# Writing each engine's order of work out as a list, in place of priorities that a small scheduler weighs

## The chip, the cores and the metric

One Trainium2 chip, one core. The metric is the device time of one execution in microseconds (us), smaller is better. In the profile PE is the engine of the matmuls, PEld its weight loads, DVE, ACT and POOL are the vector, scalar and GpSimd engines, and SP issues transfers; SPq is SP's transfer queue. The span of a trace runs from its first to its last instruction; in the kernels timed here the measured time is 1.8 to 2.1 us more than the span (median of each kernel's executions).

## The reference, cut to what matters

```python
# attention part: 4 batches, 8 heads, 768 steps, 48 wide
f = 1 / (1 + exp(-f_logit))
for t in range(S):
    state = f[t] * state + outer(k[t], v[t])
    y[t]  = q[t] @ state
# MLP part: x = y as 3072 tokens of 384
h   = x @ w_in                       # 384 -> 2048
g   = 0.5 * (h + sqrt(h*h + 4))
out = g @ w_out                      # 2048 -> 384
```

All inputs and the output are float32; the kernel multiplies in float16.

## The kernel before

It cuts the 3072 steps into 24 blocks of 128 steps, two blocks to a pair, 12 pairs. For each pair it loads f, q, k and v (eight loads of 192 KB), takes logs of the decays, sums them with matmuls, takes exponentials, multiplies q and k by them, transposes, and makes scores, states and y. Then y is transposed and goes through the two layers of the MLP: "first-layer" groups (M1: 6 matmuls, then a square and, for two groups together, one root on ACT, then the gate on DVE) and "second-layer" quarters (M2). The weights come in eight pieces each of w_in and w_out, issued by POOL between its own products and casts.

ACT needs another table of functions for exponentials than for roots (the trace has twelve table loads of 1.28 us; around the one at 57.68 us a root ends at 57.66 and the exponential starts at 58.97), so it works in stretches of one kind.

Every piece of work is an `Op` with an engine, its needs and the code that emits it. A small model of the chip runs in the builder and decides in what order each engine's instructions are written down. In the kernel before, it chooses among what is ready by a due time, made of one number per pair and part and one per kind:

```python
BASE = {
    "A": [108.49, 34.87, 152.35, -8.64, ...],        # logs, decays, q*e, k*e, casts
    "B": [-110.5, 81.39, 112.94, 46.29, ...],        # attention
    ...
    "L": [-402.69, -47.56, -326.02, -208.05, ...],   # loads
}
SHIFT = {"ldf": -73.74, "ldq": 12.88, ..., "pin": -578.98, "pout": -533.94, ...}
NEAR = {'PE': 0.02, 'ACT': 0.05, 'DVE': 0.2, 'POOL': 0.3, 'SP': 0.1}
# [...]
    def run(self):
        # [...] cands: the first op of every queue of the engine, with the time it could start
                t0 = min(c[0] for c in cands)
                near = [c for c in cands if c[0] <= t0 + NEAR.get(eng, 0.05)]
                c = min(near, key=lambda c: c[1].due)
```

Transposes are done by PE for the early pairs and by a transfer that transposes for the later ones, both of q and k (`qkT`) and of y (`xT`, the input of the first layer).

```python
                def yx():
                    xn()
                    nc.sync.dma_start_transpose(out=xo(), in_=T["y16", r].rearrange("p a b -> p (a b)"))
                op = P.add("xy", "SP", 1.2, yx, deps=[yc_op], p=p, due=due + 6.0, ...)
```

These transposes stand in the same queue of SP as the loads.

## Time and profile before

| | before |
|---|---|
| time, median of 3 executions | 207.05 us (206.78 to 207.27) |
| span of the profiled execution | 205.7 us (that execution took 207.66 us) |
| busy: PE, ACT, DVE, POOL | 180.6, 168.9, 144.0, 90.7 us |
| mean transfer rate over the span | 156 GB/s |

The lines that carry the argument are shown in the prediction: the busy table and slices, unbroken runs of matmuls, and the chain of waits from 15 to 45 us.

### The profile page before, as it was taken

What the parts mean: (1) busy time and instruction counts of PE and PEld (TensorE: products, weight loads), DVE (VectorE), ACT (ScalarE), POOL (GpSimd) and SP (SyncE); (2) the same over time, 40 slices, a digit from 0 to 9 for tenths busy, and PEclk for the clock granted to TensorE, in tenths of its full rate; (3) what the DMA queues carried; (4) which work ended last, traced back from release to release, by engine and by line L of the source; (5) the groups of instructions that cost most, each with busy time, mean ns of one, the idle gap of its engine ahead of it and who ended that gap; (6) DMA issues with size and microseconds to landing.
All of it is one profiled execution on the core that took longest, in us unless ns stands there. A gap on an engine that the chain in (4) does not pass through costs nothing.

```text
span 205.7 us, 4831 instructions
## 1 busy us (share of the span) xinstructions
PE 180.6 (88%) x1870; PEld 131.7 (64%) x1870; DVE 144.0 (70%) x286; ACT 168.9 (82%) x271; POOL 90.7 (44%) x103
## 2 busy tenths in 40 slices
PE   0666588769898998999999999999989999999993
PEld 0343365557676576777777777677757777767751
DVE  5856276778765768998598984989718988943720
ACT  5457217979999999999999999999879899967930
POOL 7171699990049396309960059900079100010010
PEclk9999996999999999999999999999999999999999
DMA  7999999999799999999999897998967712031112
GB/s 129 189 186 184 183 189 183 201 201 191 134 208 212 188 214 188 197 178 223 207 163 217 139 206 147 202 184 170 195 138 153 132 36 62 21 96 41 38 38 76
DMA packets 128102, 32.09 MB, mean 156 GB/s; under 512 B 121088, under 2 KB 127360, under 8 KB 128080
## 3 DMA queue, kind: packets, MB, share of 16 engines
q1 hardware_dynamic: 121744, 25.70, 74.4%
q0 software_dynamic: 6336, 6.10, 15.2%
q8 instruction: 14, 0.23, 0.5%
q14 instruction: 8, 0.07, 0.1%
HBM read 25.17 MB, written 4.72 MB: 145 GB/s over the span
## 4 chain that ended last, share of the span: by engine, by line
PE 60%; ACT 11%; DMA 9%; SPq 7%; POOL 5%; issue 3%; DVE 3%; DVEq 0%; ACTq 0%; POOLq 0%
PE o L777 26%; PE hps L734 23%; SPq L376 7%; ACT r L749 4%; DMA w_in<-in_moe_w_in_dram 4%; ACT hsq L740 3%; DMA ld_q<-in_q_dram 3%; PE sc L612 3%; DMA xT<-y 2%; POOL w_in L400 2%; PE y L635 1%; PE u L700 1%; PE y L633 1%; ACT ld_f L422 1%; PE u L697 1%
## 5 line engine op out<-in xcount | busy, mean ns | idle before, releaser
L734 PE MATMUL hps<-xT,w_in 128*128 128x256 f16 x576 | 72.3, 276 | 2.6 <-DMA w_in<-in_moe_w_in_dram 2.0
L757 DVE SCALAR_TENSOR_TENSOR g<-hps,r 128x512 f16<-128x512 f32 x96 | 62.1, 685 | 17.4 <-ACT r L749 16.6
L777 PE MATMUL o<-w_out,g 128*128 128x384 f16 x384 | 72.3, 326 | 0.9 <-DVE o_sb L788 0.8
L734 PEld LDWEIGHTS <-w_in 128*128 128x128 f16 x576 | 55.1, 99 | 14.0 <-DMA w_in<-in_moe_w_in_dram 3.0
L740 ACT ACTIVATE hsq<-hps 128x512 f16<-128x512 f32 x96 | 54.0, 591 | 6.8 <-PE hps L734 5.5
L749 ACT ACTIVATE r<-hsq 128x1024 f16<-128x1024 f16 x48 | 50.8, 1057 | 1.4
L777 PEld LDWEIGHTS <-g 128*128 128x128 f16 x384 | 35.3, 97 | 20.2 <-issue 1.3
L619 DVE TENSOR_TENSOR pm<-sc,mask 128x512 f16<-128x512 f32 x48 | 31.3, 683 | 8.8 <-PE sc L612 8.6
L792 POOL DMA_DIRECT2D out_dram<-o_sb x15 | 8.6, 571 | 59.1 <-DVE o_sb L788 43.4
L484 POOL TENSOR_TENSOR qk<-ld_q,ea 128x768 f16<-128x768 f32 (+1 forms) x10 | 15.7, 1571 | 27.1 <-PE hps L471 14.2
L484 POOL TENSOR_TENSOR qk<-ld_k,eap 128x768 f16<-128x768 f32 (+1 forms) x12 | 18.6, 1546 | 0.7 <-ACT eap L478 0.6
L433 POOL TENSOR_TENSOR llo<-ls,lhi 128x768 f16<-128x768 f32 (+1 forms) x12 | 16.8, 1399 | 2.0 <-PE hps L734 1.5
L491 POOL CAST v<-ld_v 128x768 f16<-128x768 f32 (+1 forms) x13 | 8.8, 682 | 18.5 <-DMA ld_v<-in_v_dram 17.6
L704 DVE TENSOR_TENSOR sn<-u,gam 128x384 f16<-128x384 f32 x20 | 11.0, 551 | 7.3 <-PE u L700 6.7
L422 ACT ACTIVATE ld_f<-ld_f 128x768 f32<-128x768 f32 (+1 forms) x15 | 10.8, 723 | 4.6 <-DMA ld_f<-in_f_logit_dram 4.5
L478 ACT ACTIVATE ea<-hps 128x384 f32<-128x384 f32 x24 | 10.9, 500 | 4.1 <-PE hps L471 4.0
L464 PE MATMUL hps<-lhi,wcent 128*128 128x384 f16 x24 | 8.7, 361 | 6.1 <-POOL lhi L430 5.4
L635 PE MATMUL y<-v,pm 128*128 128x48 f16 x192 | 12.0, 189 | 1.0 <-DVE pm L619 1.0
L635 PEld LDWEIGHTS <-pm 128*128 128x128 f16 x192 | 10.4, 100 | 2.9 <-DVE pm L619 1.1
L612 PE MATMUL sc<-qkT 48*128 48x128 f16 x192 | 10.6, 233 | 1.8 <-DVE qkT L591 0.8
L587 PE MATMUL tr<-ident,qk 128*128 128x128 f16 x80 | 7.8, 256 | 4.7 <-POOL qk L484 4.3
L427 ACT ACTIVATE ls<-ld_f 128x768 f32<-128x768 f32 (+1 forms) x15 | 10.7, 715 | 1.0
(55 smaller groups left out, 209.0 us busy)
## 6 DMA issues: line engine op xcount, KB each, us to landing
ld_f<-in_f_logit_dram SPq DMA_DIRECT2D x24, 192.0 KB, 4.6
ld_k<-in_k_dram SPq DMA_DIRECT2D x24, 192.0 KB, 4.6
ld_q<-in_q_dram SPq DMA_DIRECT2D x24, 192.0 KB, 4.4
ld_v<-in_v_dram SPq DMA_DIRECT2D x24, 192.0 KB, 4.3
out_dram<-o_sb POOLq DMA_DIRECT2D x15, 192.0 KB, 3.6
out_dram<-o_sb SPq DMA_DIRECT2D x9, 192.0 KB, 2.0
w_in<-in_moe_w_in_dram POOLq DMA_DIRECT2D x8, 192.0 KB, 7.1
w_out<-in_moe_w_out_dram POOLq DMA_DIRECT2D x8, 192.0 KB, 7.9
```

Of the source, the lines that this page charges most:

```text
L376: (nc.gpsimd if cast else nc.sync).dma_start(out=T["v16" if cast else name, p][:, r], in_=src_of[name][b][:, c * C:(c + 1) * C, :].rearran ...
L422: nc.scalar.activation(out=f, in_=f, func=AF.Exp, scale=-1.0)
L433: eng_of[lg[p, x].eng].tensor_tensor(out=llo[p % NL][:, x:y, :, 0:D], in0=T["ls", p][:, x:y], in1=lhi[p % NL][:, x:y, :, 0:D], op=ALU.subt ...
L484: eng_of[mu[p, x, i].eng].tensor_tensor(out=qk[p % NB][:, x:y, i, :, 0:D], in0=T[name, p][:, x:y], in1=T[e, p][:, x:y], op=ALU.mult)
L612: nc.tensor.matmul(out=T["sc", r, s][:, j, :], lhsT=qkT[o:o + D, NP + j, :], rhs=qkT[o:o + D, j, :], start=True, stop=True)
L619: nc.vector.tensor_tensor(out=T["pm", r][:, s], in0=T["sc", r, s], in1=mask16.unsqueeze(1).broadcast_to([128, NP, C]), op=ALU.mult)
L635: nc.tensor.matmul(out=y[:, j, s], lhsT=T["pm", r][:, s, j, :], rhs=T["v16", p][:, i, 2 * j + s, :], start=(c == 0), stop=(c == 0 or s == 1))
L734: nc.tensor.matmul(out=hb[:, a, :], lhsT=w_in16[j2][:, j, a * 128:(a + 1) * 128], rhs=T["xT", p][:, j, :], start=(j == 0), stop=(j == NJ - 1))
L740: nc.scalar.activation(out=T["hsq", p, j4][:, a], in_=T["h", p, j2], func=AF.Square, scale=1.0)
L749: nc.scalar.activation(out=T["r16", p, j4], in_=T["hsq", p, j4], func=AF.Sqrt, scale=0.25, bias=1.0)
L757: nc.vector.scalar_tensor_tensor(out=T["g", p][:, jn:jn + 2, :].rearrange("p a t -> p (a t)"), in0=T["h", p, 2 * j4 + a], scalar=0.5, in1= ...
L777: nc.tensor.matmul(out=T["o", p, i], lhsT=T["g", p][:, jn, i * C:(i + 1) * C], rhs=w_out16[jn // 2][:, jn % 2, :], start=(jn == 0), stop=( ...
```

## The change

The intent: no due times any more. Each engine has a string with one letter for each piece of work, and the model only works out where that puts every piece in time. The strings were searched directly, against two sets of modelled transfer and instruction times.

```diff
-BASE = { "A": [108.49, 34.87, ...], ... }
-SHIFT = { "ldf": -73.74, ... }
-NEAR = {'PE': 0.02, 'ACT': 0.05, 'DVE': 0.2, 'POOL': 0.3, 'SP': 0.1}
+NAME = {
+    "W": "W", "h": "hi", "l": "lo", "k": "qk", "v": "v16", ... "1": "M1", "m": "M", "r": "R", "g": "G",
+    "2": "M2", "e": "ev", "o": "out", "F": "ldf", "Q": "ldq", "H": "ldk", "V": "ldv", "i": "pin", "u": "pout",
+}
+TAKE = {
+    "PE": "WWTSTWSWYKTSYTKtStKYWYWttT11SK1K1Y1111T1t1S11211Y1t1..."   [...]
+    "POOL": "hlkkkhhvlvkkkvhiivlliiiiikkviuuuluuuuuvkholookkhvv..."   [...]
+    "SP": "VFFFQHQVHFVQHHHFQFHVQQVVFQFFVVHHFFQQQVFHHHFqqVVHHqyyQqQQqqyFFyVqoqy...",
+}
 [...]
-                t0 = min(c[0] for c in cands)
-                near = [c for c in cands if c[0] <= t0 + NEAR.get(eng, 0.05)]
-                c = min(near, key=lambda c: c[1].due)
+                k = (eng, NAME[take[place[eng]]])
+                op = self.queues[k][heads[k]]
```

In SP's string F, Q, H, V are the loads of f, q, k, v (one block each for the first three pairs, a pair of blocks after that), q is a transpose of q and k, y one of y, and o a store. In POOL's, i and u are the pieces of w_in and w_out. Two further edits: the wait of the weight pieces on earlier ones and on casts is gone (the list's order holds it now), and the engine of some casts, products and copies is another.

## The prediction

> **What bounds the kernel now.** I read the page first: its busy table, then the 40 slices.
>
> ```profile
> PE 180.6 (88%) x1870; PEld 131.7 (64%) x1870; DVE 144.0 (70%) x286; ACT 168.9 (82%) x271; POOL 90.7 (44%) x103
> ...
> PE   0666588769898998999999999999989999999993
> ...
> ACT  5457217979999999999999999999879899967930
> ...
> DMA  7999999999799999999999897998967712031112
> ```
>
> PE and ACT are both close to full from about slice 10 on (a slice is 5.14 us); before that neither is, and the DMA engines are. So there are two regimes. Busy matmul time is a soft measure, so I asked how much real work PE does in each stretch. The chain of waits has long unbroken runs that give the price of one matmul:
>
> ```profile
> 186.51 2.62 PE hps L734 x24
> ...
> 194.35 7.81 PE o L777 x48
> ```
>
> That is 0.109 us for a first-layer matmul (256 columns) and 0.163 us for a second-layer one (384 columns). The other kinds I priced in the same way, start to start, in PE's timeline after 30 us: 0.162 us for a 384-column decay matmul, 0.026 for its two-column companions, 0.041 for a score, 0.056 for a transpose, about 0.02 to 0.05 for the small state and output matmuls. Multiplying by the counts per window of the windows view gives PE's real work: 8.1 us in 0 to 30, 8.2 in 30 to 45, 4.9 in 45 to 50, 36.9 in 50 to 90, 60.5 in 90 to 150, 9.4 in 150 to 160, 42.7 in 160 to 203: 170.6 us in all. One window as an example, all PE matmuls, then the two layers alone:
>
> ```profile
> 170.00:180.00 10.00, 10.00 (x113) 7.76 (x111) 9.06 (x16) 9.73 (x15) 0.00 (x0) 1.00 0.17 43
> ...
> 170.00:180.00 10.00, 6.12 (x50) 4.62 (x48) 1.00 0.17 43
> ...
> 170.00:180.00 10.00, 3.42 (x18) 1.52 (x18) 1.00 0.17 43
> ```
>
> 50 x 0.109 + 18 x 0.163 = 8.4 us, and the other 45 small matmuls bring it to 10.1: PE is truly full there. So PE loses 28.7 us before 45 us, about 3.9 us between 45 and 203 (3.1 of it between 50 and 90, 0.6 between 150 and 160), and the last 3.5 us are the last eviction and store. **Almost all that an order can win lies in the first 45 us.**
>
> What rules there? The chain in that window:
>
> ```profile
> 15.89 5.60 DMA ld_q<-in_q_dram
> ...
> 21.62 1.00 POOL qk L484
> ...
> 25.91 0.87 POOL llo L433
> 26.78 0.45 POOL v L491
> 27.23 1.22 POOL w_in L400 x2
> ...
> 36.61 0.77 POOL lhi L430
> 37.38 7.39 DMA w_in<-in_moe_w_in_dram
> 44.76 0.05 issue
> ```
>
> Inputs arrive one by one (about 1.03 us each, DMA full), POOL multiplies and casts them, only then issues the weights, and the eighth w_in piece, issued at 37.38, lands at 44.76. From then PE is full. Its last matmuls of the first pair of blocks waited for just that.
>
> **What the Trainium skill says.** "Perfetto Trace Analysis", section "Identifying the Most-Contended Engine": matmul busy time is no measure of distance from the limit, since matmuls are pipelined. The trace agrees: in 40 to 90 us busy time looks fuller than the work counted. "TensorE: Matmul & The Clock Gate", Part 1: PE is at half clock until it has been kept busy. The trace agrees in the durations, though its clock row reads full: two decay matmuls follow each other at 0.32 us at 7.7 us and 0.16 at 55 us, and the change falls near 29 us. As data is what is missing there, I count this as a symptom. "DMA: Bandwidth & Descriptors", "Issuing engines are not separate DMA queues": POOL's and SP's transfers interleave on the same 16 engines. It agrees: the eight w_in pieces take 4.3, 6.1, 6.9, 7.9, 6.9, 8.3, 7.4, 7.4 us to land, beside input loads. "ScalarE: Activation LUTs", "What ACT_TABLE_LOAD costs": 1283 ns a load; the trace has twelve of 1283 ns.
>
> **The change, part by part.** It is order, and little else. I compared the instruction orders of the two built programs.
> (a) Removed or added work: none on PE (the same matmuls); the twelve table loads stay. The transposes through DMA stay for pairs 5 to 11 (the old list's larger numbers name no pair). Engine moves: one qkT copy goes from ACT (1.01 us) to DVE (0.69) and one y eviction the other way, so ACT has 0.5 us less; casts and products moved between DVE and POOL cancel within half a microsecond by their rows' durations; one store goes from POOL to SP. Sum: nothing on a path.
> (b) The bulk. ACT's division into stretches is literally the same: 9, 2, 5, 8, 8 and 16 roots between the same exp stretches. Before the 16th, 24th, 32nd... first-layer group PE has done 2, 16, 21, 33, 37, 49, 54, 64, 69, 76, 84 second-layer quarters before, and 1, 16, 20, 32, 37, 49, 54, 65, 68, 77, 85 after. So this is a local rearrangement. As PE is full there, it can return at most the 3.9 us lost after 45; I give it 1.3, about a third, because some of those gaps have the DMA or ACT behind them.
> (c) The first 25 loads are reordered: before, blocks of f, k, q, v of whole pairs; now block by block. Loads land, by place in the queue (issue start plus time to landing, before): place 11 at 15.3 us, 12 at 16.3, 16 at 21.5, 19 at 24.2, 21 at 26.2, 23 at 28.4. The third block's q goes from place 16 to 11 and its k stays at 12; the fourth block's v goes from place 21 to 19; in exchange a v is first and f comes 1.1 us later.
> (d) POOL and DVE divide the first block otherwise. Following the new order by the durations of before (POOL product 1.00, cast 0.50, difference 0.90, weight issue 0.80): the first block loses about 1.7 us (three products in a row on POOL, transpose at 10.4 instead of 8.75), then waits for data anyway. The third block's products end at 18.7 instead of 24.5, its transposes start at 18.7 instead of 22.67. The fourth block's v is cast at 24.7 instead of 27.2, after it one cast, and the first w_in is issued at 25.2 instead of 27.18: 2.0 us earlier. Then a cast and two differences stand ahead of the third w_in (29.7 against 28.9), five issues follow to 33.7, two products and a cast, and the eighth goes at 36.2 instead of 37.38. The w_out pieces go 1.3 to 3 us earlier.
> (e) The landing. From 31.5 to 44.76 seven w_in pieces landed, one per 1.9 us, and the w_out ones after them 1.3 to 1.6 us apart: a stream limited by DMA share, so its start and its last issue both count. Started 2.0 us and ended 1.2 us earlier, I put the eighth at 43.0 instead of 44.76. At that point the new order has 0.6 us less other PE work done (one transpose group, one back-transpose). Net 1.2 us, to which I add 0.7 for the earlier w_out and the fuller stretch behind: **1.9 us**.
> Sum: 1.9 + 1.3 = 3.2 us off 205.7. The measured time is 1.35 us over the traced span (207.05 against 205.7), so about 203.9 us.
>
> **The rivals.** *The load queue is the bound of the start and order cannot help*: DMA is at 9 tenths from slice 2 on, and the w_in pieces share it with loads; if the earlier weights only push loads back, the eighth lands at 44.5 and the time is 205.5 to 207. For it: the slow landings of 7 to 8 us. Against it: the weight stream did start late, behind POOL's products. *The search found more than I can follow by hand*: the 28.7 us of loss are large, and if PE is kept at work with second-layer quarters or the clock is up by 22 us, 5 to 7 us go: 200 to 202. For it: PE waits 3.5 us at 22.67 alone. Against: ACT's stretches and the counts in (b) are those of before. *A new wait*: a fixed order searched on modelled times may sit at the head of an engine with work that comes late (POOL's products against its weight issues, SP's transposes against loads). Each slip stops a full PE; 1 to 4 us back, 206 to 209. The two sets of times in the search speak against it. *ACT becomes the bound*: it has 168.9 us and some 10 us of slack after 45, so not for a gain of this size.
>
> **Range and chances.** My steps give 203.9; the head's term is uncertain by 2 us either way and the bulk's by 1.5, which with rounding makes 200.8 to 206.8 for 8 in 10. Faster by over 2% means below 202.9: 0.36. Slower by over 2% means above 211.2: 0.03. Within: 0.61.
>
> **What would show it.** Same work: PE's 1870 matmuls and twelve table loads. Step (d): third block's transposes near 18.7, the first w_in issue near 25, the eighth near 36. Step (e): PE full from about 43. Step (b): counted PE work short by 2 to 3 us instead of 3.9 after that point. The prediction is wrong if PE fills before 41 or not before 45, or if new gaps over 1 us stand in PE's timeline after 50 us.

## More of the kernel before

One more view is needed, which the prediction did not look at closely enough: the timeline of ACT just after 46 us. Its columns are start, duration, engine, line, operation, tiles and, in brackets, the idle time before.

```profile
46.30 1.06 ACT L749 ACTIVATE r<-hsq 128x1024 f16<-128x1024 f16 x1
47.27 1.06 ACT L740 ACTIVATE hsq<-hps 128x512 f16<-128x512 f32 x2
48.37 1.06 ACT L749 ACTIVATE r<-hsq 128x1024 f16<-128x1024 f16 x1
49.33 1.06 ACT L740 ACTIVATE hsq<-hps 128x512 f16<-128x512 f32 x2
```

A root, two squares, a root, two squares, 2.06 us a round and next to no idle time. Exponentials and table loads come between such rounds later on, but from here to 92 us the view of waits has no wait of ACT at all, and it is busy 97 to 98% of the time. ACT sets the pace there, not PE.

## The result

| | before | after |
|---|---|---|
| median of 4 executions each, same rounds | 206.92 us (206.48 to 207.27) | 205.75 us (205.64 to 205.85) |
| span of the profiled execution | 205.7 us | 203.5 us |

The ratio is 0.9945, with a 95% interval of 0.9924 to 0.9965: faster by half a per cent, which counts as the same at a threshold of 2%. A ratio here is the mean time of one kernel's executions over that of the other's of the same rounds, so not quite the ratio of the medians. The changed kernel is clearly faster, but by 1.2 us where 3.15 us were forecast.

The page of the changed kernel, the busy table and three rows of slices:

```profile
PE 179.4 (88%) x1870; PEld 131.4 (65%) x1870; DVE 141.1 (69%) x286; ACT 167.9 (83%) x271; POOL 91.5 (45%) x102
...
PE   0576849679987999999999998999999999999993
...
ACT  3674416999999999999989997999989997898840
...
DMA  6999999999999999999999998999809673221112
```

A slice is 5.09 us here. The same 1870 matmuls; but look at PE's row for digits under 9 from the tenth slice on, the stage where the prediction expected less loss. There is an 8 and a 7 at 56 to 66 us and one 8 at 122 to 127 us. Both will be named below, and they turn out to be of very different worth. The head went as forecast. POOL's timeline of the changed kernel, the weight issues:

```profile
25.30 1.71 POOL L339 DMA_DIRECT2D w_in<-in_moe_w_in_dram  x2
...
29.68 3.87 POOL L339 DMA_DIRECT2D w_in<-in_moe_w_in_dram  x5
...
35.93 0.80 POOL L339 DMA_DIRECT2D w_in<-in_moe_w_in_dram  x1
```

The first piece goes at 25.3 us (before 27.2, forecast 25.2), the eighth at 35.9 (37.4, forecast 36.2), and it lands at 42.8 (44.8, forecast 43.0). The third block's transposes on PE begin at 17.7 us and their second half at 18.65 (before at 22.7, forecast 18.7). ACT's fourth root shows what that is worth:

```profile
43.69 0.60 ACT L677 ACTIVATE hsq<-hps 128x512 f16<-128x512 f32 x1 [0.35 <-PE hps L671]
44.32 1.06 ACT L686 ACTIVATE r<-hsq 128x1024 f16<-128x1024 f16 x1
```

44.32 us against 46.30 before: a lead of 2.0 us. As both kernels do the same 48 roots in the same stretches, the start of the n-th root is a good clock, and I use it from here on. The table gives, for some roots, when the kernel before started them in the trace of the last section, and how much earlier (minus) or later (plus) the other traces did. The columns other than "after" are experiments, told below. The new list puts other work between some roots, so single roots swing (the 38th is 2.5 us early, the 42nd only 0.2); what is meant to last has to show in several of them.

| root | before, us | after | e0c (old order again) | e2 | e4 | e5 | e6 |
|---|---|---|---|---|---|---|---|
| 4th | 46.3 | -2.0 | -0.2 | -1.8 | -2.0 | -1.3 | +1.9 |
| 10th | 66.7 | -2.0 | -0.2 | -1.2 | -2.0 | -1.3 | +1.9 |
| 13th | 82.6 | -2.1 | -0.2 | -0.5 | -2.2 | -1.3 | +1.6 |
| 22nd | 112.5 | -2.0 | -0.1 | -0.9 | -2.2 | -1.3 | +1.7 |
| 25th | 129.0 | -0.7 | -0.1 | -0.9 | -2.0 | -1.3 | +1.8 |
| 34th | 158.1 | -1.8 | -0.9 | -1.6 | -2.8 | -2.1 | +1.1 |
| 46th | 190.5 | -2.1 | -0.9 | -1.6 | -3.2 | -2.1 | +0.7 |

The lead of 2.0 us is there from the fourth root on and *nothing* is added in the 66 us that follow. Then 1.3 us of it are lost between the 22nd and the 25th root. The chain of waits of the changed kernel shows where:

```profile
118.46 0.65 PE o L713 x4
119.11 4.54 DMA xT<-y
123.69 2.13 PE hps L671 x18
```

A first-layer group waits for a transpose of y that was issued at 119.11 and landed 4.5 us later. PE finds 0.82 us of idle time there, and PE's work counted at the prediction's prices is 9.19 us between 120 and 130 us, against 9.98 before. SP's timeline says why the transpose was issued so late:

```profile
114.50 1.42 SPq L604 DMA_TRANSPOSE xT<-y  x1
116.02 3.00 SPq L315 DMA_DIRECT2D ld_f<-in_f_logit_dram  x4
119.11 1.88 SPq L604 DMA_TRANSPOSE xT<-y  x1
```

y was ready at about 115.9 us, but four loads of f, which took 3.0 us to issue, stood ahead of it in the list, and the two transposes of q and k ahead of those had begun only at 110.8, after the queue had been idle for 1.8 us (the issues before ended at 109.0). ACT, too, stands still there, for one of these loads of f:

```profile
123.27 0.84 ACT L360 ACTIVATE ld_f<-ld_f 128x768 f32<-128x768 f32 x1 [0.90 <-DMA ld_f<-in_f_logit_dram]
```

That is the rival "a new wait" of the prediction, and it had happened; the lead seems to come back later (-1.8 at the 34th root), but that is the kernel before losing time of its own in this trace, at 150 us:

```profile
151.61 1.47 PE L734 MATMUL hps<-xT,w_in 128*128 128x256 f16 x12 [0.61 <-DMA xT<-y]
```

So the theory to be tested: **the head gains 2.0 us as forecast; the rest gains nothing, because ACT sets the pace to 90 us and PE was full already after it; and a new wait at 119 us takes 1 us back.** The rivals: the head's gain is not what counts (the rest would have caught up or fallen back anyway); PE's other new wait, 2.0 us at 60 us, is what costs; it is ACT's wait for f that costs, not PE's for the transpose; or more than 1 us was never there, the profiled execution of before being a slow one.

### The profile page after: what moved, and what is told of

The parts are those of the page before. It is cut to its first block, busy times and chain, and to the rows that moved or that the text cites. A ratio compares the mean times of both kernels' runs of the same rounds, so it can differ in the third digit from the quotient of the medians.

```text
span 203.5 us, 4839 instructions
## 1 busy us (share of the span) xinstructions
PE 179.4 (88%) x1870; PEld 131.4 (65%) x1870; DVE 141.1 (69%) x286; ACT 167.9 (83%) x271; POOL 91.5 (45%) x102
## 4 chain that ended last, share of the span: by engine, by line
PE 55%; SPq 23%; DMA 9%; ACT 6%; issue 2%; POOL 2%; DVE 1%; POOLq 0%; ACTq 0%
PE o L713 23%; SPq L315 23%; PE hps L671 22%; DMA ld_f<-in_f_logit_dram 4%; PE sc L549 2%; DMA xT<-y 2%; DMA ld_k<-in_k_dram 2%; ACT hsq L677 2%; DMA ld_v<-in_v_dram 2%; ACT r L686 2%; PE y L572 1%; PE hps L402 1%; PE y L570 1%; PE hps L403 1%; POOL qk L422 1%
## 5 line engine op out<-in xcount | busy, mean ns | idle before, releaser
L713 PE MATMUL o<-w_out,g 128*128 128x384 f16 x384 | 70.9, 326 | 0.0
L671 PEld LDWEIGHTS <-w_in 128*128 128x128 f16 x576 | 54.5, 99 | 13.0 <-DMA w_in<-in_moe_w_in_dram 2.8
L728 POOL DMA_DIRECT2D out_dram<-o_sb x14 | 7.9, 567 | 42.6 <-ACT o_sb L722 37.8
L422 POOL TENSOR_TENSOR qk<-ld_k,eap 128x768 f16<-128x768 f32 (+1 forms) x12 | 19.9, 1655 | 15.9 <-ACT eap L416 8.9
L429 POOL CAST v<-ld_v 128x768 f16<-128x768 f32 (+1 forms) x14 | 10.2, 736 | 17.3 <-DMA ld_v<-in_v_dram 16.6
L403 PE MATMUL hps<-llo,wcent 128*128 128x384 f16 x24 | 8.8, 368 | 3.6 <-POOL llo L371 3.5
L581 DVE CAST y<-y 128x384 f16<-128x384 f32 x15 | 8.2, 551 | 4.8 <-PE y L572 4.7
L524 PE MATMUL tr<-ident,qk 128*128 128x128 f16 x80 | 8.6, 264 | 3.2 <-POOL qk L422 3.0
```

The lines of the kernel that those rows point to most:

```text
L422: eng_of[mu[p, x, i].eng].tensor_tensor(out=qk[p % NB][:, x:y, i, :, 0:D], in0=T[name, p][:, x:y], in1=T[e, p][:, x:y], op=ALU.mult)
L671: nc.tensor.matmul(out=hb[:, a, :], lhsT=w_in16[j2][:, j, a * 128:(a + 1) * 128], rhs=T["xT", p][:, j, :], start=(j == 0), stop=(j == NJ - 1))
L713: nc.tensor.matmul(out=T["o", p, i], lhsT=T["g", p][:, jn, i * C:(i + 1) * C], rhs=w_out16[jn // 2][:, jn % 2, :], start=(jn == 0), stop=( ...
```

## The experiments

All kernels gave correct results. "Before" was timed in the same rounds in each batch: 206.74 us for e0 to e3 (206.25 to 207.97), 206.73 for e4 to e6, 206.85 for e7 to e9 (11 executions each). The median span of before is 204.7, 204.7 and 204.9 us. Each batch ran on another chip, so kernels of different batches are compared through before.

### e0: the old order written as lists

To take single parts of the change over I first needed the old order in the new form. The lists were taken from the order that the old builder had put out; the order of instructions on each engine is identical.

```diff
-        "VFFFQHQVHFVQHHHFQFHVQQVVFQFFVVHHFFQQQVFHHHFqqVVHHqyyQq..."    # SP, after
+        "FFHHQQVVFFFFHHHHQQQQVVVVFHQFFVHHFFQQVVHHQQFFqqVVHyHqyQ..."    # SP, old order; the other engines likewise
```

> The kernel before with its own order written out as lists, instruction for instruction the same on every engine. Every theory: ratio 1.000 within 0.002 of the kernel before. It is a second trace of the order before: if the profiled execution of the kernel before (207.66 us, median 206.92) was simply a slow one, this trace has a span near 205.0 instead of 205.7, and the 2.2 us between the two profiles shrink to about the 1.1 us that the medians show. If instead the span is 205.7 again, the profiles' difference is real and the medians hide it.

207.04 us, ratio 1.0011 (0.9981 to 1.0042). The form costs nothing, and parts may be exchanged.

### e2 and e3: new head with old rest, old head with new rest

Cut where the engines stand at about 45 us.

```diff
# e2, the string of SP (the other engines likewise)
-        "VFFFQHQVHFVQHHHFQFHVQQVVFQFFVVHHFFQQQVFHHHFqqVVHHqyyQqQQqqyFFyVq..."
+        "VFFFQHQVHFVQHHHFQFHVQQVVFQFFHVHHFFQQVVHHQQFFqqVVHyHqyQqqQFyFqoyV..."
# e3
-        "VFFFQHQVHFVQHHHFQFHVQQVVFQFFVVHHFFQQQVFHHHFqqVVHHqyyQqQQqqyFFyVq..."
+        "FFHHQQVVFFFFHHHHQQQQVVVVFHQFFVVHHFFQQQVFHHHFqqVVHHqyyQqQQqqyFFyVq..."
```

> The changed kernel's order up to about 45 us (through the last weight transfer), the order of the kernel before from there on. Theory that the whole gain is made in the head: as fast as the changed kernel, 205.4 to 206.1. Theory that the rest matters as well (the prediction gave it 1.3 us): about 1 us slower than the changed kernel, near 206.7.

205.93 us, ratio 0.9960 (0.9927 to 0.9993).

> The order of the kernel before up to about 45 us, the changed kernel's order from there on. Theory that the gain is made in the head: as the kernel before, 206.6 to 207.2. Theory that the rest brings something of its own: 205.6 to 206.2. If the rest of the new order is worse than the old on its own: above 207.4.

206.15 us, ratio 0.9977 (0.9942 to 1.0011).

The new head alone gives 0.8 us, the new rest alone 0.6 us with an interval that includes nothing, both together 1.2. In e2 the lead is 1.8 us at the fourth root and shrinks to 0.5 at the 13th: the old rest can't hold it. ACT waits 0.18 us for PE at 48.4 us and 0.45 us at 80.8, and its rounds take 2.17 us from 49 to 54 us, so with the old rest PE's groups come too late for an ACT that is ahead. In the changed kernel the lead is held at 2.0. So the new rest is of use after all: it keeps what the head has won up to 112 us, and then loses 1 us of it. Its net worth on top of the new head is 205.93 - 205.75 = 0.2 us, or 0.4 us by the differences to before (0.81 and 1.17): neither can be told from zero.

e3 shows on what the loss depends. From 45 us on it has the changed kernel's lists, and it issues the same transpose at 119.53 us behind the same loads, but PE has no wait for it:

```profile
124.18 2.14 PE L671 MATMUL hps<-xT,w_in 128*128 128x256 f16 x18
```

PE comes to this group 0.5 us later than it could start in the changed kernel (123.69). The queue moved forward with the new head by 0.4 us only (119.11 against 119.53), so its late transpose limits how much of a lead can pass.

### e1: the load that PE waits for at 60 us, moved forward

In the changed kernel PE stands still for 2.0 us for a product of k of the fourth pair. PE's timeline:

```profile
62.32 0.84 PE L524 MATMUL tr<-ident,qk 128*128 128x128 f16 x12 [2.01 <-POOL qk L422]
```

That load of k stood behind two loads of v in SP's list.

```diff
-        "VFFFQHQVHFVQHHHFQFHVQQVVFQFFVVHHFFQQQV..."
+        "VFFFQHQVHFVQHHHFQFHVQQVVFQFFHVVHFFQQQV..."
```

> The changed kernel with one load moved: the k load of the fourth pair is issued before the two v loads instead of after them. Theory that the late k (landing at 60.3 us, PE idle 2.0 us for it) gave back part of the gain: 1 to 2 us faster than the changed kernel, 204 us. Theory that ACT paces that stretch and PE makes up for the gap behind it: PE's gap at 60 us goes but the time stays within 0.4 us of the changed kernel, 205.4 to 205.8.

206.0 us, ratio 0.9960 (0.9931 to 0.9990), so no gain on the 205.75 of the changed kernel. In its trace the idle time is 0.91 us instead of 2.01, and PE's counted work between 60 and 70 us is 8.59 us instead of 7.77. That the edit did this is not shown: e4 below, which leaves these loads as they are, had only 0.7 us of this wait in its trace, so its size changes from one execution to another. What the wait is worth can be read from the roots all the same. From the ninth root, before it, to the 24th the lead grew by 0.15 us in the changed kernel with 2.01 us of the wait, and by 0.31, 0.32 and 0.30 us in e1, e4 and e9 with 0.91, 0.7 and 0.96. So 1.1 to 1.3 us less idle time of PE moved ACT by less than 0.2 us. While ACT sets the pace, PE's idle time is all but free.

### e4: the late transpose moved ahead of the loads of f

The one disputed wait, taken away by moving the work it waits behind: one load of f (one F of the list, two of the four transfers) goes ahead of the two transposes of q and k into the idle time of the queue, and the transpose of y goes ahead of the other.

```diff
-        "...VVHHqyyQqQQqqyFFyVqoqyVyqVq..."
+        "...VVHHqyyQqQQFqqyyFVqoqyVyqVq..."
```

> The changed kernel with two moves in the transfer queue near 115 us: one f load goes ahead of two transposes (the queue is idle there), and the transpose of a finished y goes ahead of the other f load instead of behind both. In the changed kernel PE and ACT lose about 1.2 us of their lead there, PE waiting for that transpose. Theory that this is a new wait of the searched order and that PE sets the end from 90 us on: the wait at 123 us goes and the kernel is 0.6 to 1.0 us faster than the changed kernel, about 205.0 (ratio to the kernel before 0.991). Theory that the slack behind it absorbs it, as it did with the k load: no change, 205.6 to 206.0.

**204.80 us, ratio 0.9914 (0.9880 to 0.9949)**: better than both kernels. Against the changed kernel the medians differ by 0.95 us and the median spans by 1.05 (203.8 and 202.75); the ratios, 0.9914 against 0.9945, by only 0.6 us, as one of e4's six executions took 206.64 us, an outlier that stays unexplained. The two were timed in different batches, each beside before. SP's timeline of e4:

```profile
114.35 2.62 SPq L604 DMA_TRANSPOSE xT<-y  x2
117.06 1.16 SPq L315 DMA_DIRECT2D ld_f<-in_f_logit_dram  x2
```

Both transposes are issued by 117 us, no wait of PE for `xT` is left in the trace, PE's counted work between 120 and 130 us is 10.01 us, and the lead at the 25th root is 2.0 us where it was 0.7. From the 28th root to the end e4 is 1.0 us ahead of the changed kernel at every root looked at: the late transpose costs about 1 us.

The edit also moved a load of f, and ACT's wait for f is gone as well, so e4 alone does not say which of the two waits cost the time. e1's trace does. ACT has no wait for f in it, and PE has the one for `xT`:

```profile
123.92 2.12 PE L671 MATMUL hps<-xT,w_in 128*128 128x256 f16 x18 [0.88 <-DMA xT<-y]
```

Against e9, which is e1 with the edit of e4, it is 0.2 us behind at the 24th root and 1.15 us from the 28th to the end; the medians are 206.00 and 204.76 us. PE's wait is enough to explain the loss.

### e5 and e6: the order of the first loads alone, and the new order without it

```diff
# e5: the old order, with the first 24 loads of the new
-        "FFHHQQVVFFFFHHHHQQQQVVVVFHQFF..."
+        "VFFFQHQVHFVQHHHFQFHVQQVVFHQFF..."
# e6: the changed kernel, with the first 24 loads of the old order
-        "VFFFQHQVHFVQHHHFQFHVQQVVFQFFVV..."
+        "FFHHQQVVFFFFHHHHQQQQVVVVFQFFVV..."
```

> The kernel before with only its first 24 loads in the new order. Theory that the order of loads alone starts the weights earlier: first w_in issue near 25.6 us instead of 27.2, the eighth near 36, ACT ahead by 1 to 1.7 us at its fourth root, time 0.5 to 1 us under the kernel before. Theory that the new division of the first blocks between POOL and DVE is needed as well: issues and time as before within 0.3 us.

206.00 us, ratio 0.9962 (0.9939 to 0.9985). The first weight piece goes at 26.0 us, the eighth lands at 43.4, and the lead is 1.3 us in its trace, of which 0.7 us show in the median time.

> The changed kernel with its first 24 loads put back into the old order. Theory that the order of loads is what starts the weights earlier: first w_in issue near 27 us again, ACT no longer ahead at its fourth root, time within 0.4 us of the kernel before. Theory that the division of work carries it: first issue at 25 to 26 us and the time of the changed kernel.

208.22 us, ratio 1.0064 (1.0044 to 1.0085): slower than before by 1.5 us. POOL's timeline of e6:

```profile
24.74 0.50 POOL L429 CAST v<-ld_v 128x384 f16<-128x384 f32 x1 [7.83 <-DMA ld_v<-in_v_dram]
...
29.12 1.71 POOL L339 DMA_DIRECT2D w_in<-in_moe_w_in_dram  x2
```

POOL's list puts the cast of a v first that the old load order brings ten places later (the 21st load, where it is the 11th in the new order; the prediction counts places from nought); POOL stands still for 7.8 us with all the weights behind it. So the order of loads carries 1.3 of the 2.0 us of lead, and the new order of POOL and DVE works only together with it. A list that was written for one order of loads does not adapt to another; the old builder would have chosen again by its model.

### e0b, e7 and e0c: the wait of the kernel before at 150 us

Three traces of the old order (205.7, 205.6 and in e0b 205.3 us of span) all lay above its median span of 204.7. e0b was one look more at the old order:

> A third trace of the old order. The two so far have spans of 205.7 and 205.6 us, the median of the executions of the kernel before is 204.7. If this one falls near 204.7, the milestones of its trace (fourth root, first-layer groups) show where a fast execution gains 0.9 us on a slow one: in the head, if it is DMA timing. If it is slow again there is nothing to see.

207.33 us in that one execution, with the wait for `xT` near 151 us at 0.3 us instead of 0.6, and from there on 0.3 us of lead over the first trace. e7 took what stands ahead of that transpose away: a load of q, moved behind it.

```diff
# the old order, SP
-        "...FyFqoyVyoVqqyHqHyQqoQVyVyoqqyqqyyoyyoooo"
+        "...FyFqoyVyoVqqyHqHyQqoVyVQyoqqyqqyyoyyoooo"
```

> The kernel before with one q load moved behind the transpose that PE and ACT wait for near 150 us, so that the two v loads leave earlier. Theory that the kernel before had a wait of its own there, which the new order lost by other neighbours, and which comes and goes with the run: PE's wait for xT near 151 us goes, the time is 0.4 to 0.8 us under the kernel before (206.0 to 206.4), and ACT's lead at the last third is like that of the hybrid with the old head (1.3 us less the head's part). Theory that it is noise: within 0.2 us of the kernel before.

206.63 us, ratio 0.9992 (0.9975 to 1.0009): no gain that can be told from zero, though in its trace the wait was gone and the 34th root came 1.0 us earlier than in the first trace. The two fit together only if most executions of the old order do not have the wait. e0c, a last look at the old order, was to tell:

> One more trace of the old order, the fourth. The three so far were slow executions of it (spans 205.7, 205.6, 205.3 against a median of 204.7), all with a wait of the PE for a transpose near 150 us (0.61, 0.6 and 0.3 us). Theory 1 (that wait is what differs between the executions of the old order): if this one has a span of 205.0 or less, its waits near 150 are gone and ACT's roots after 155 us come 0.8 to 1.0 us earlier than in the first trace, with no change before 140. If the span is 205.3 or more, the wait is there again. Theory 2 (the difference arises elsewhere, as in the landing of the first loads): the roots shift at 46 us or before, and the wait near 150 stays.

206.74 us, span 204.8: a usual execution this time. PE's timeline, around the group that had waited:

```profile
148.74 2.11 PE L713 MATMUL o<-w_out,g 128*128 128x384 f16 x12
150.69 1.47 PE L671 MATMUL hps<-xT,w_in 128*128 128x256 f16 x12
```

It starts at 150.69 with no idle time before it (151.61 with 0.61 us in the first trace), and the table shows the whole difference between the two executions of one order arise there: -0.1 at the 25th root, -0.9 at the 34th. In SP's timelines the transposes and loads between 136 and 146 us were simply issued a little faster, 2.20 us for one at 136.34 against 3.05 for the same one:

```profile
136.34 2.20 SPq L604 DMA_TRANSPOSE xT<-y  x1
```

So the profiled execution of before was 0.9 us longer than this one for a wait that comes and goes. It looks like the rarer case: 26 of the 33 executions of before in the three batches have spans of 205.2 us or less. Why a queue issues faster in one execution than in another, no run here shows.

### e9: the two edits of e1 and e4 together

```diff
-        "...FQFFVVHHFFQQQVFHHHFqqVVHHqyyQqQQqqyFFyVq..."
+        "...FQFFHVVHFFQQQVFHHHFqqVVHHqyyQqQQFqqyyFVq..."
```

> The changed kernel with the transpose freed near 115 us and the k load ahead of the v loads. Theory that ACT paces 45 to 90 us and only waits behind 90 us count: PE's gap at 60 us goes, time as without this move, 204.5 to 205.1. Theory that the two waits add up: 203.8 to 204.3.

204.76 us, ratio 0.9908 (0.9884 to 0.9931), the same as e4. This does not test the wait at 60 us, as was meant: it is 0.96 us in e9's trace and was already 0.7 in e4's. It does repeat the gain of e4's edit, on e1.

### e8: weights ahead of a cast, on top of e4

Could the head win more? Before the first weight piece POOL waits for a load of v. Three pieces were put ahead of that cast, and one more ahead of the next cast of v.

```diff
-        "hlkkkhhvlvkkkvhiivlliiiiikkviuuu..."
+        "hlkkkhhvlvkkkiiivhivlliiikkviuuu..."
```

> The changed kernel with the transpose freed near 115 us, and three of the w_in issues moved ahead of the v cast for which POOL idles from 21.7 to 24.4 us, a fourth ahead of the next cast. Theory that the start is bound by the landing of the eighth w_in piece and POOL issues it late: first issue near 21.8, eighth near 35, landing 41 to 42 instead of 42.8, ACT 0.6 to 1.5 us further ahead at its fourth root, time near 204.0. Theory that the DMA engines are full and bytes are bytes: the loads land later in exchange, the fourth root is not earlier than in the kernel without this move, time 204.6 to 205.4.

**208.63 us, ratio 1.0076 (1.0052 to 1.0099)**, slower than e4 by 3.8 us. The first piece did go earlier, at 21.8 us. SP's timeline for the same two loads of v, first in e4:

```profile
23.12 1.71 SPq L315 DMA_DIRECT2D ld_v<-in_v_dram  x2
```

then in e8, with the weights beside them, and POOL's timeline of e8 with the cast that waits for the first of them:

```profile
23.38 3.98 SPq L315 DMA_DIRECT2D ld_v<-in_v_dram  x2
...
33.04 0.50 POOL L429 CAST v<-ld_v 128x384 f16<-128x384 f32 x1 [6.86 <-DMA ld_v<-in_v_dram]
...
35.23 2.32 POOL L339 DMA_DIRECT2D w_in<-in_moe_w_in_dram  x3
```

The loads took 9.6 and 8.8 us to land where e4's took 4.2. POOL stood still for 6.9 us with the other four w_in pieces behind that cast, and the eighth landed at 46.5 us, where e4's had at 42.8; ACT is 4.2 us behind e4 from its fourth root to the end. This is the rival "the load queue is the bound of the start", seen from its other side: the weights can start early only as far as they do not push back loads that POOL's own list needs next.

## Why the prediction was wrong

- **Step (a), no change of work.** Held: 1870 matmuls, the same 48 roots, and about one us less on ACT (167.9 against 168.9).
- **Steps (c), (d) and (e), the head, 1.9 us.** Held: issues at 25.3 and 35.9, landing at 42.8, lead 2.0 us. The landing came 2.0 us earlier (forecast 1.8), and the lead is just that. The 0.6 us that (e) then took off and the 0.7 it added nearly cancel, and no run tests them, so that 1.9 meets 2.0 so well is in part luck. e5 adds that 1.3 of the lead is the loads' order, e6 that the rest of it depends on that order.
- **"From then PE is full", and PE full from 43 to 45.** Wrong. Between 45 and 90 us ACT works almost without a gap and PE does not (counted work 7.8 us of 10 between 60 and 70 in the changed kernel), and 1.1 to 1.3 us less idle time of PE there moved ACT by less than 0.2 (e1, e4, e9). The rival "ACT becomes the bound" was dismissed with slack summed over the whole span after 45 us, though it holds in this stage.
- **Step (b) is the one that failed: "it can return at most the 3.9 us lost after 45; I give it 1.3, about a third".** Most of those 3.9 us (3.1 by the prediction's own count) lay between 50 and 90 us, where ACT sets the pace and PE's losses are all but free, and the lead there stayed at 2.0. Of the 0.6 us between 150 and 160, the old order in its usual execution loses nothing (e0c). So nothing was added to the head's lead. Instead about 1.0 us of it was lost at 119 us, which e4 gave back. On top of the lead the term was -1.0, not +1.3.
- **The sum of the two terms.** It let each stand alone, and they do not. Without the new rest the head's lead mostly goes (e2: 0.8 us of time are left), and the wait at 119 us is there only when the head is ahead (e3). Counted by exchange, the new rest is worth 0.6 us on the old head, 0.2 to 0.4 on the new one, and 1.1 on the new one with the late transpose moved (e4 against e2): it keeps a lead, it does not make one.
- **The sign "new gaps over 1 us in PE's timeline after 50 us".** One came, of 2.0 us at 60 us, and was worth next to nothing. The one that cost 1 us was 0.82 us long.
- **The rival "a new wait"** was the right one, in the very form it had: a transpose behind loads in SP's list. Its size, "1 to 4 us back", was at the low end. It was counted as an alternative to the gain of the head, though the two add up.
- **The offset.** "The measured time is 1.35 us over the traced span" took a span from one execution (207.66 us) and a time from the median of others (207.05). Within one execution the difference is about 1.97 us. This put the forecast 0.6 us too low.

In the change from before to after: forecast 3.15 us, that is 1.9 from the head and 1.3 from the rest; measured 1.17 us, about 2.0 from the head less 1.0 at the new wait. With the wait gone (e4) 1.93 us are measured, about the head's lead. What stays open is which piece of the old order makes PE's groups late between 46 and 82 us (e2), and why the waits at 60 and at 150 us change from one execution to another.

## What to carry to other kernels

Ask of each stage which engine never waits in it, before pricing what another engine loses there: here over 1 us of PE's idle time was worth less than 0.2 us, and a wait of under 1 us in a later stage was worth all of its length. When orders are fixed by a list, look through the queue of transfers for short transfers that a full engine waits for, standing behind loads that nobody needs yet; moving one such transpose forward, and one load out of its way, won nearly as much as the whole search had (0.95 us against 1.17). And take the distance between time and span, and the size of small waits, from more than one execution: one and the same wait was 2.0 us in one trace and 0.7 in another.

## What the Trainium skill lacked or had wrong

- "VectorE: DVE Perf Modes", section "The three transpose paths", gives one figure for a transpose through DMA, 1309 ns for 128x128 of bf16. In the changed kernel the transposes of y (128x384 of float16) took 2.3 to 4.9 us from issue to landing, in the middle 3.2, and the one that cost 1 us took 4.5 with loads ahead of and behind it in its queue. What matters for an order is that spread; it is on no page that I read.
- "DMA: Bandwidth & Descriptors", section "Issuing engines are not separate DMA queues", says that transfers of all engines interleave, which the traces agree with, but not what that costs the other stream: four weight pieces issued ahead moved the landing of two loads from 4.2 us to 9.6 and 8.8 (e4 and e8), and the kernel by 3.8 us.
- "Perfetto Trace Analysis", section "Optimization Strategy", says rightly that a kernel can have several regimes with other most-contended engines, and to look for gaps in the regime of interest. A sentence is lacking on what the gaps of another engine are worth in such a regime: over 1 us of PE's idle time at 60 us, where ACT sets the pace, was worth less than 0.2 (e1, e4, e9).
- No page that I read gives a figure for how much whole executions of one kernel differ: the spans of the old order went from 204.2 to 206.0 us, and 0.9 us of that was one wait that was there or not (e0c).
